# A new instruction order for pooled attention with two MLPs, and weight conversion held in SBUF

## The chip, the cores and the metric

The kernel runs on one core of a Trainium2 chip. The time is device microseconds of one execution, the median of several runs. PE is the matrix engine (TensorE), DVE is VectorE, ACT is ScalarE, POOL is GpSimd, and SP issues the transfers.

## The reference, cut to what matters

```python
# q (12288, 128), kv (384, 32, 128), w_sr (128, 128), all float32
kv_pool = kv.reshape(1, 96, 4, 8, 4, 128).mean(axis=(2, 4))    # 4x4 pooling: 768 keys
k = v = kv_pool.reshape(1, 768, 128) @ w_sr
s = (q @ k.T) / sqrt(128);  a = softmax(s);  x = a @ v         # x (12288, 128)

h = x @ moe_w_in                                               # (128, 2048), float64 in HBM
g = where(h >= 1, h, where(h <= -1, 0, (h + 1)**2 / 4))
x = g @ moe_w_out                                              # (2048, 128), float64 in HBM

h = x @ moe2_w_in
return (h * (1 / (1 + exp(-1.702 * h)))) @ moe2_w_out
```

The four MLP weights arrive as float64 and are turned into pairs of 32-bit values (a high part and the rest) on the chip.

## The kernel before

**Stages.** The 12288 queries are cut into 24 blocks of 512. At the start twelve chunks of kv of 512 KB are loaded (L265), four rows summed by DVE (even chunks, L277) or POOL (odd chunks, L280 and L281), and multiplied by a pooling matrix on PE (L294). The last two chunks, 10 and 11, are split: one half is summed by DVE, the other goes to PE unsummed in eight small matmuls (L292). The pooled keys, 768 columns in two halves of 384, are copied by ACT (L338), multiplied with w_sr (L343), and split into two parts kT by ACT (L350) and DVE (L210). The second half is done in two pieces: 256 columns that need chunk 9, and 128 columns that need chunk 11. Values are made by L368 and L376. While kv loads, PE also runs matmuls on a tile of zeros (`warm`, L320): 36 of 256 columns at the start and 7 after each of nine chunks.

**A block.** A block's attention is scores S (L214 to L216, six matmuls of 384 columns per tile of 128 queries), maximum (L523), exponential (L536), and the product with the values. Blocks 0 to 3 turn the probabilities on PE (L585) and multiply in plain float32 (L599); the others turn them by DVE and HBM. Then each MLP takes the 16 groups of 128 hidden columns in eight pairs: six matmuls into h, some elementwise work, a high part `ghi` by ACT and a rest `glo` by POOL (L210) or DVE, six matmuls into acc. In MLP 1 the elementwise work is a clip (L788 on DVE, or L786 on ACT where the block's digit in `LIGHT` isn't 0), a square (L795 on ACT, or L793 on POOL where the digit is 1) and L799 on DVE. MLP 2 uses two activations (L828, L834); its `glo` goes to DVE for the pairs named in `LOW_DVE` (pair 4 of every block).

**Weights.** Sixteen units of 128x512, four for each of W1, O1, W2, O2, are loaded (512 KB each) and converted (function `unit`): an absolute value on ACT into a tile `i`, a clamp (L413), a shift (L417), a sign (L421) and a tail (L428) on DVE, a high part on ACT (L435) and the rest on POOL (L210). Tile `i` lies in PSUM, in the one buffer of the room `accB`, and the result `f` of the tail in SBUF, in the room `o`, which has two buffers.

**The order.** Nothing is reordered at run time. `Plan` places every task with a list scheduler when the program is built: each engine, when it comes free, takes the ready task with the lowest key whose buffers ("rooms") are free. Keys and assumed durations are numbers in the code. The order that comes out is written into each engine's stream, and the engine keeps to it. Room `h` has three buffers of PSUM, shared by the scores, the transposes, the h of both MLPs, the key products and `warm`. The clamp of every weight unit is placed after all of kT (`after=[a, *kT_done]`).

Of the kernel before, what the change touches and what calls it, by code (L numbers as in the profile page):

```python
# [17 lines left out]
PSUM = bass.MemoryType.PSUM  # L18

# [111 lines left out]
def tile_pooled_attention_two_mlps(  # L131
# [40 lines left out]
    MM, MMS, MMF = 0.2273, 0.173, 0.224  # L172
# [4 lines left out]
    ATT_AT, ATT_GAP, REG_AT = ((-84.9, 56.1, 67.6, 104.1), ((2.4, 7.7), (8.6, 4.4), (9.6, 0.3), (2.5, 2.3)), 2.93)  # L177
    STEP_AT = (0.54, 2.45, 0.5)
    ATT_KEY = (26.49, 2.85, 18.08, 13.03, -19.64, 10.84, 4.1, -15.3, 8.86, 57.26, -2.82)
    PAIR1 = (3.65, -0.48, 3.27, 7.62, -6.74)  # L180
    PAIR2 = (1.57, -6.31, 2.52, 13.5)
    ENDS = (7.48, -5.42)
    V_AT = (-50, -16.8)
    LEAD = (-6.4, -20.7)
    LOW_DVE = (4,)
    LIGHT = ('12010111', '02111000', '22200000')
# [16 lines left out]
    def hold(room):  # L203
        return Hold(R[room])

# [22 lines left out]
    warm = sb.tile([P, 256], BF16, name="warm")  # L228
# [27 lines left out]
    pool_mm = [None] * NPC  # L256
    kv_rooms = ["u"] * 4 + ["hi"] * 4 + ["lo"] * 4
    pool_hold = [hold("accA"), hold("accB")]
    for i in range(NPC):
# [39 lines left out]
        if i >= NPC - 2:  # L299
            s = add("DVE", 1.05, -90 + i, lambda i=i, yh=yh: sums(nc.vector, i, yh, slice(0, 1)), after=[t], takes=[yh], uses=[h])  # L300
            direct = add("PE", 0.8, -90 + i, lambda i=i, f=pooled: f(i, [1], True), after=[t, c_t], uses=[h, ph])
            pool_mm[i] = add("PE", 0.23, -90 + i, lambda i=i, f=pooled: f(i, [0]), after=[s, c_t, direct], uses=[yh, ph])
        else:
            whole = slice(0, GP)
            if i % 2 == 0:
                s = add("DVE", 1.92, -90 + i, lambda i=i, yh=yh: sums(nc.vector, i, yh, whole), after=[t], takes=[yh], uses=[h])
            else:
                s = add("POOL", 2.05, -90 + i, lambda i=i, yh=yh: sums(nc.gpsimd, i, yh, whole), after=[t], takes=[yh], uses=[h])
            pool_mm[i] = add("PE", 0.45, -90 + i, pooled, after=[s, c_t], uses=[yh] + ([] if first else [ph]),
                             takes=[ph] if first else [])  # L310
# [3 lines left out]
    for i in range(NPC - 2):  # L314

        def work(i=i):
            if i == 0:
# [4 lines left out]
        add("PE", 5.0 if i == 0 else 0.43, 300, work, after=[w_t] if i == 0 else [pool_mm[i - 1]],  # L322
            uses=[warm_h] if i else [], takes=[] if i else [warm_h])
# [5 lines left out]
    def k_part(c0, c1, after):  # L329
        half = c0 // HALF  # L330
        fresh = c0 % HALF == 0
        r = slice(c0 % HALF, (c1 - 1) % HALF + 1)
        n = c1 - c0

        def copy():
            if fresh:
                pT_t[half] = slot(pT_h[half], [P, HALF], F32, "pT", "hi")
            nc.scalar.activation(pT_t[half][:, r], pool_ps[half][:, r], AF.Copy)  # L338

        def mult():  # L340
# [4 lines left out]
        a = add("ACT", act_us(n), -70 + half, copy, after=[after], uses=[pool_hold[half]] + ([] if fresh else [pT_h[half]]),  # L345
                takes=[pT_h[half]] if fresh else [])
        m = add("PE", 0.05 + n / 600, -80 + half, mult, after=[a, wsr_t], uses=[pT_h[half]] + ([] if fresh else [kps_h[half]]),
                takes=[kps_h[half]] if fresh else [])
        hi = add("ACT", act_us(n), -70 + half,
                 lambda: nc.scalar.activation(kT[0][:, c0:c1], kps_t[half][:, 0, r], AF.Copy), after=[m], uses=[kps_h[half]])  # L350
        lo = add("DVE", dve_us(n), -70 + half,
                 lambda: split_lo(nc.vector, kT[1][:, c0:c1], kps_t[half][:, 0, r], kT[0][:, c0:c1]),
                 after=[hi], uses=[kps_h[half]])
        kT_done.append(lo)
        kmul[half].append(m)
        return a
# [35 lines left out]
    def unit(name, src, j, rows, key, load_key, f_room):  # L392
# [32 lines left out]
        def tail():  # L425
            fi, raw = T["i", name, j].bitcast(I32), T["raw", name, j]
            f = T["f", name, j] = slot(fh, [P, TB], F32, "f")
# [14 lines left out]
        a = add("ACT", act_us(TB), key - 5, absolute, after=[d], uses=[rh], takes=[ih])  # L442
        b = add("DVE", 0.69, key - 4.5, clamp, after=[a, *kT_done], uses=[ih])
        c = add("DVE", 0.69, key - 4, shift, after=[b], uses=[ih])
        e = add("DVE", 0.69, key - 3.5, sign, after=[c], uses=[ih, rh])
        g = add("DVE", 0.69, key - 3, tail, after=[e], uses=[ih, rh], takes=[fh])
        hi = add("ACT", act_us(TB), key - 2, high, after=[g], uses=[fh], takes=[wh])
        lo = add("POOL", 1.3, key - 1, low, after=[hi], uses=[fh])
# [9 lines left out]
    for j in range(NW):  # L458
        unit("W1", w_in1, j, False, at(2 * j) - 2 - LEAD[0], -60 + 2 * j, "accB")
        unit("O1", w_out1, j, True, at(2 * j + LAG_O) - LEAD[0], -59 + 2 * j, "accB")  # L460
    for j in range(NW):
        unit("W2", w_in2, j, False, at(NP + LAG_B + 2 * j) - LEAD[1], -40 + 2 * j, "accB")
        unit("O2", w_out2, j, True, at(NP + LAG_B + LAG_O + 2 * j) - LEAD[1], -39 + 2 * j, "accB")

# [9 lines left out]
    def q_prep(b, key):  # L474
# [25 lines left out]
        d = add("SP", 2.0, key - 20 if b else -77, load, takes=[rh])  # L500
        a = add("DVE", 0.62, key - 5, turn, after=[d], uses=[rh], takes=[th, hh, lh])
        h = add("ACT", act_us(TB), key - 4, high, after=[a], uses=[th, hh])
        lo = add("POOL" if b else "DVE", 1.3 if b else 0.69, key - 3, low, after=[h], uses=[th, lh])
# [6 lines left out]
    def scores(b, t, key, ph=None, ahead=(1.0, 2.0, 2.5)):  # L510
# [3 lines left out]
        def S_mm():  # L514
            S = T["S", b, t] = psum(sh, f"S{b}_{t}")
            cols = [T[n, b][:, t * P : (t + 1) * P] for n in ("qhi", "qlo")]
            for half in range(2):
# [26 lines left out]
        m = add("PE", 6 * MMS, key, S_mm, after=[*kT_done, *q_done[b]], takes=[sh], uses=q_hold[b])  # L544
# [18 lines left out]
    def early(b, base, gap, gap2):  # L563
# [8 lines left out]
        def by_tile(n, t0, t1):  # L572
            return T[("pv", "spread", "rds")[n], b].rearrange("p (i t b) -> p i t b", i=4, b=32)[:, :, t0:t1, :]
# [201 lines left out]
    def pair1(b, k, a):  # L775

        t0 = at(a)
        hh, m = h_pair(1, b, k, t0)
# [38 lines left out]
        o_pair(1, b, k, at(a + LAG_O) + STEP_AT[1] * STEP, [hi, lo], [ih, lh])  # L817

    def pair2(b, k, a):

        t0 = at(a) + STEP_AT[0] * STEP
        hh, m = h_pair(2, b, k, t0)
        uh, ih, lh = hold("u"), hold("hi"), hold("lo")
        on_dve = k in LOW_DVE
# [24 lines left out]
        o_pair(2, b, k, at(a + LAG_O) + STEP_AT[2] * STEP, [hi, lo], [ih, lh])  # L849
# [79 lines left out]
```

## Time and profile before

| | |
|---|---|
| median of 3 runs | 1316.44 us (1315.85 to 1320.16) |
| the profiled execution: span from the first to the last instruction | 1315.1 us |
| PE busy | 1296.3 us (99%) |
| DVE, ACT, POOL busy | 932.6, 1089.0, 937.0 us |

The profiled execution has no time of its own beside its span; the median of the runs is 1.3 us longer than the span. PE is the engine to follow: its idle time, and work on it that serves nothing, are what a change of order can touch.

### The profile page before, as it was taken

To read this page: it belongs to the slowest core of one execution; us is meant where nothing else is said; L and a number is where in the kernel's file an instruction comes from. 1 tells how busy PE (TensorE), PEld (TensorE's weight loads), DVE (VectorE), ACT (ScalarE), POOL (GpSimd) and SP (SyncE) were. 2 spreads that over 40 slices of the span, in tenths; PEclk is the share of its full clock that TensorE was granted. 3 is DMA by queue.
4 is the path that set the end of the run, shared out by engine and by line. 5 is a ranking of instruction groups with operands and counts; after the bars stand their busy time and mean duration, and the time that the engine had idled before them with its cause. 6 is when DMAs were issued, how large, how long until landed. Compare 5 with 4: busy or idle time off the path is not lost.

```text
span 1315.1 us, 17281 instructions
## 1 busy us (share of the span) xinstructions
PE 1296.3 (99%) x6025; PEld 1088.1 (83%) x6025; DVE 932.6 (71%) x1196; ACT 1089.0 (83%) x1260; POOL 937.0 (71%) x427
## 2 busy tenths in 40 slices
PE   8899999999999999999999999999999999999998
PEld 7688788888888888888888888888888888888886
DVE  5887587777768777777777677777776877775531
ACT  2888888988888889888888898898888888987765
POOL 3577876776777667667767777677677766767886
PEclk8999999999999999999999999999999999999999
DMA  9400045534543454455345534554454345433000
GB/s 329 146 16 9 1 112 168 137 110 148 136 127 104 137 153 127 113 167 134 107 124 147 144 106 112 168 137 112 147 137 125 104 140 152 118 104 99 6 8 16
DMA packets 166309, 154.30 MB, mean 117 GB/s; under 512 B 108240, under 2 KB 153424, under 8 KB 166224
## 3 DMA queue, kind: packets, MB, share of 16 engines
q1 hardware_dynamic: 165168, 153.07, 41.2%
q8 instruction: 49, 0.80, 0.3%
q14 instruction: 36, 0.29, 0.1%
q10 hardware_dynamic: 1056, 0.13, 0.1%
HBM read 83.95 MB, written 69.21 MB: 116 GB/s over the span
## 4 chain that ended last, share of the span: by engine, by line
PE 95%; DVE 2%; DMA 1%; ACT 1%; issue 0%; POOL 0%; SPq 0%; DVEq 0%; ACTq 0%; POOLq 0%
PE acc L767 13%; PE acc L765 13%; PE acc L764 13%; PE h L214 13%; PE h L215 13%; PE h L216 13%; PE S L214 2%; PE S L216 2%; PE S L215 2%; PE pv L216 2%; PE pv L214 2%; PE pv L215 2%; PE pv L599 2%; DMA kv<-in_kv 1%; PE T L585 1%; DVE mx L523 0%
## 5 line engine op out<-in xcount | busy, mean ns | idle before, releaser
L210 POOL TENSOR_TENSOR glo<-u,ghi 128x1024 fp32r<-128x1024 f32 x360 | 860.3, 2408 | 303.5 <-ACT ghi L805 135.1
L788 DVE TENSOR_SCALAR u<-h 128x1024 f32<-128x1024 f32 x179 | 219.4, 1225 | 197.6 <-PE h L216 184.7
L764 PE MATMUL acc<-ghi,O 128*128 128x512 f32 x768 | 300.4, 391 | 0.0
L765 PE MATMUL acc<-ghi,O 128*128 128x512 f32 x768 | 299.6, 390 | 0.0
L799 DVE SCALAR_TENSOR_TENSOR u<-h,u 128x1024 f32<-128x1024 f32 x192 | 233.2, 1215 | 85.7 <-ACT u L795 80.9
L828 ACT ACTIVATE ghi<-h 128x1024 fp32r<-128x1024 f32 x192 | 197.2, 1027 | 71.4 <-PE h L216 70.7
L767 PE MATMUL acc<-glo,O 128*128 128x512 f32 x768 | 237.6, 391 | 0.0
L795 ACT ACTIVATE u<-u 128x1024 f32<-128x1024 f32 x184 | 194.5, 1057 | 31.7 <-DVE u L788 31.2
L805 ACT ACTIVATE ghi<-u 128x1024 fp32r<-128x1024 f32 x192 | 203.3, 1060 | 9.7 <-DVE den L540 3.9
L834 ACT ACTIVATE u<-h 128x1024 f32<-128x1024 f32 x168 | 171.2, 1020 | 0.0
L767 PEld LDWEIGHTS acc<-glo,O 128*128 128x128 f32 x768 | 144.0, 188 | 31.2 <-POOL glo L210 0.4
L765 PEld LDWEIGHTS acc<-ghi,O 128*128 128x128 f32 x768 | 144.2, 188 | 27.8
L764 PEld LDWEIGHTS acc<-ghi,O 128*128 128x128 f32 x768 | 144.1, 188 | 26.8
L214 PE MATMUL h<-xhi,W 128*128 128x512 f32 x384 | 150.3, 392 | 5.2 <-ACT xhi L556 2.3
L215 PE MATMUL h<-xlo,W 128*128 128x512 f32 x384 | 149.8, 390 | 0.2 <-DVE xlo L210 0.2
L214 PE MATMUL h<-x2hi,W 128*128 128x512 f32 x384 | 149.7, 390 | 0.1
L216 PE MATMUL h<-xhi,W 128*128 128x512 f32 x384 | 149.7, 390 | 0.0
L215 PE MATMUL h<-x2lo,W 128*128 128x512 f32 x384 | 149.4, 389 | 0.0
L216 PE MATMUL h<-x2hi,W 128*128 128x512 f32 x384 | 149.4, 389 | 0.0
L523 DVE TENSOR_REDUCE mx<-S 128x1 f32<-128x768 f32 x96 | 91.5, 953 | 8.7 <-PE S L216 6.4
L214 PEld LDWEIGHTS h<-xhi,W 128*128 128x128 f32 x384 | 72.1, 188 | 22.4 <-issue 2.5
L215 PEld LDWEIGHTS h<-xlo,W 128*128 128x128 f32 x384 | 72.1, 188 | 15.7 <-DVE xlo L210 0.5
(94 smaller groups left out, 1835.3 us busy)
## 6 DMA issues: line engine op xcount, KB each, us to landing
turned<-TT SPq DMA_DIRECT2D x80, 768.0 KB, 4.2
PT_hi<-turned SPq DMA_DIRECT2D x160, 192.0 KB, 3.8
PT_lo<-turned SPq DMA_DIRECT2D x160, 192.0 KB, 4.6
kv<-in_kv SPq DMA_DIRECT2D x12, 512.0 KB, 7.8
q<-in_q SPq DMA_DIRECT2D x96, 64.0 KB, 2.4
out<-o SPq DMA_DIRECT2D x94, 64.0 KB, 1.9
raw_W<-in_moe_w_in SPq DMA_DIRECT2D x8, 512.0 KB, 9.6
raw_O<-in_moe_w_out SPq DMA_DIRECT2D x8, 512.0 KB, 9.4
```

Of the source, the lines that this page charges most:

```text
L210: eng.tensor_tensor(out=lo, in0=full, in1=f32(hi), op=ALU.subtract)
L214: nc.tensor.matmul(ps, wl, xh, start=first, stop=False)
L215: nc.tensor.matmul(ps, wh, xl, start=False, stop=False)
L216: nc.tensor.matmul(ps, wh, xh, start=False, stop=last)
L764: nc.tensor.matmul(acc, w[c][1], hi[:, c], start=k == 0 and c == 0, stop=False)
L765: nc.tensor.matmul(acc, w[c][0], hi[:, c], start=False, stop=False)
L767: nc.tensor.matmul(acc, w[c][0], lo[:, c], start=False, stop=k == NP - 1 and c == 1)
L788: nc.vector.tensor_scalar(u, T["h", 1, b, k], -1.0, 1.0, ALU.max, ALU.add)
L795: nc.scalar.activation(u, u, AF.Square, scale=1.0 if light else 0.5)
L799: nc.vector.scalar_tensor_tensor(out=u, in0=T["h", 1, b, k], scalar=1.0, in1=u, op0=ALU.max, op1=ALU.min)
L805: nc.scalar.activation(t, T["u", b, k], AF.Copy)
L828: nc.scalar.activation(t, T["h", 2, b, k], AF.Gelu_apprx_sigmoid)
```

## The change

- All keys are moved into a table `ORDER`, and many have new values; some lists now have values for each of the first three to six blocks. Early attention has the keys (-143.62, 2.8, 71.1, 121.75) where it had (-84.9, 56.1, 67.6, 104.1).
- While kv loads: `warm` has 512 columns; 16 matmuls run at the start, 3 after each of the first nine chunks, and 2 after the direct matmuls of chunk 10, with a key ahead of most other work where before it was behind all. Pooling matmuls, key copies and key products get lower keys. The half sum of chunk 11 goes to POOL.
- Block 0's q is loaded by one transfer whose runs are 512 bytes (four transfers with runs of 128 bytes before), and transposed by four PE instructions into the second bank of the `warm` tile (one DVE transpose before). Its scores are two tasks for each tile; the first needs only the first half of kT.
- In the conversion of W1 and O1 the tile `i` lies in SBUF, in the room `o`, and the tail writes over it. The clamps of units 1 and 3 of each (`"1212"`) go to POOL. W2 and O2 keep PSUM.
- `LIGHT` and `LOW_DVE` have digits for five and six blocks: 13 squares on POOL (8 before), and 12 rests of MLP 2 on DVE in blocks 0 to 5 (6 before).

```diff
+    LOW_DVE=("00111011", "00001000", "11001000", "00000000", "00000001", "01000001"),
+    CONV=("1212", "1212", "0000", "0000"),
+    LIGHT=("10010111", "01111000", "02000000", "00000010", "00001101"),
...
-    LOW_DVE = (4,)
-    LIGHT = ('12010111', '02111000', '22200000')
...
         if i >= NPC - 2:
-            s = add("DVE", 1.05, -90 + i, lambda i=i, yh=yh: sums(nc.vector, i, yh, slice(0, 1)), after=[t], takes=[yh], uses=[h])
-            direct = add("PE", 0.8, -90 + i, lambda i=i, f=pooled: f(i, [1], True), after=[t, c_t], uses=[h, ph])
+            last_eng = "DVE" if i % 2 == 0 else "POOL"
+            s = add(last_eng, 1.05, -90 + i, lambda i=i, yh=yh, e=last_eng: sums(nc.vector if e == "DVE" else nc.gpsimd, i, yh, slice(0, 1)),
+                    after=[t], takes=[yh], uses=[h])
+            direct_mm[i] = add("PE", 0.9, -120 + i, lambda i=i, f=pooled: f(i, [1], True), after=[t, c_t], uses=[h, ph])
...
-            for _ in range(36 if i == 0 else 7):
-                nc.tensor.matmul(T["warm"][:, 0, :256], warm[:, :P], warm, start=True, stop=True)
-        add("PE", 5.0 if i == 0 else 0.43, 300, work, after=[w_t] if i == 0 else [pool_mm[i - 1]],
+            for _ in range(n):
+                nc.tensor.matmul(T["warm"][:, 0], warm[:, :P], warm, start=True, stop=True)
...
+    spare(16, -95, [w_t], first=True)
+    for i in range(NPC - 3):
+        spare(3, -95, [pool_mm[i]])
+    spare(2, -95, [direct_mm[NPC - 2]])
...
+        conv = ORDER["CONV"][("W1", "O1", "W2", "O2").index(name)][j]
+        in_sb, on_pool = conv != "0", conv == "2"
         def absolute():
-            f = T["i", name, j] = slot(ih, [P, TB], F32, "i")
+            f = T["i", name, j] = slot(fh if in_sb else ih, [P, TB], F32, "i")
         def clamp():
-            nc.vector.tensor_scalar(f, f, F64_LO, F64_HI, ALU.max, ALU.min)
+            (nc.gpsimd if on_pool else nc.vector).tensor_scalar(f, f, F64_LO, F64_HI, ALU.max, ALU.min)
...
+                nc.sync.dma_start(t, q[b * TB : (b + 1) * TB, :].rearrange("(t p) c -> p t c", p=P))
+            def turn():
+                T["qT", b] = T["warm"][:, 1]
+                for t in range(NT):
+                    nc.tensor.transpose(T["qT", b][:, t * P : (t + 1) * P], T["q", b][:, t, :], ident)
...
+        if b == 0:
+            m0 = add("PE", 3 * MMS, key, lambda: S_mm(range(1)), after=[kT_done[0], *q_done[b]], takes=[sh], uses=q_hold[b])
+            m = add("PE", 3 * MMS, key, lambda: S_mm(range(1, 2)), after=[m0, *kT_done], uses=[sh, *q_hold[b]])
```

## Rows read from the trace of the kernel before

**Rows 1.** Page, busy time of each engine over the span.
```profile
PE 1296.3 (99%) x6025; PEld 1088.1 (83%) x6025; DVE 932.6 (71%) x1196; ACT 1089.0 (83%) x1260; POOL 937.0 (71%) x427
```

**Rows 2.** Windows: stretch, length, busy time by engine, granted clock, DMA share, GB/s.
```profile
40.00:50.00 10.00, 7.52 (x45) 6.01 (x42) 7.32 (x12) 5.70 (x10) 4.15 (x3) 1.00 0.65 181
50.00:60.00 10.00, 7.47 (x40) 6.50 (x41) 9.63 (x15) 9.21 (x13) 7.97 (x5) 1.00 0.07 11
60.00:80.00 20.00, 18.02 (x115) 15.99 (x113) 16.28 (x30) 15.97 (x24) 17.72 (x11) 1.00 0.09 14
80.00:100.00 20.00, 18.51 (x100) 15.32 (x99) 16.34 (x28) 16.48 (x25) 15.03 (x9) 1.00 0.09 14
100.00:150.00 50.00, 48.65 (x278) 41.92 (x278) 38.73 (x58) 43.20 (x58) 39.82 (x22) 1.00 0.04 6
200.00:250.00 50.00, 49.51 (x223) 41.26 (x223) 37.26 (x48) 43.09 (x49) 36.00 (x16) 1.00 0.45 119
400.00:500.00 100.00, 100.00 (x452) 84.02 (x451) 73.87 (x90) 86.14 (x98) 71.75 (x31) 1.00 0.49 135
```

**Rows 3.** Windows of one us behind the last kv chunk, same columns.
```profile
21.00:22.00 1.00, 1.00 (x7) 1.00 (x6) 1.00 (x2) 0.00 (x0) 0.00 (x0) 0.50 0.83 188
27.00:28.00 1.00, 1.00 (x8) 1.00 (x7) 0.00 (x0) 0.00 (x0) 0.00 (x0) 0.64 1.12 396
```

**Rows 4.** Timeline, kv chunks and q: start, duration, instruction, idle time before it.
```profile
10.05 5.73 SPq L480 DMA_DIRECT2D q<-in_q  x4
13.87 1.27 POOL L280 TENSOR_TENSOR z<-kv 128x512 f32<-128x512 f32 x1 [0.46 <-DMA kv<-in_kv]
16.35 1.27 POOL L280 TENSOR_TENSOR z<-kv 128x512 f32<-128x512 f32 x1 [0.40 <-DMA kv<-in_kv]
18.84 1.08 PE L292 MATMUL pool_ps<-pm,kv 128*128 128x32 f32 x8 [0.54 <-DMA kv<-in_kv]
```

**Rows 5.** Chain that ended last, from chunk 11 on: start, duration, what.
```profile
20.66 1.75 PE pool_ps L292 x8
22.44 0.39 ACT pT L338
22.87 1.22 PE k_ps L343 x2
24.36 2.99 PE warm_ps L320 x14
27.35 0.43 PE k_ps L343 x2
27.77 0.71 PE k_ps L368 x6
28.82 0.29 DVE kT L210
29.11 0.62 DVE i L413
29.75 0.70 DVE i L417
43.48 0.69 DVE i L421
```

**Rows 6.** Timeline, block 1's scores: what came before them.
```profile
46.79 0.70 DVE L487 STREAM_TRANSPOSE qT<-q 128x512 f32<-128x512 f32 x1
50.25 1.28 POOL L210 TENSOR_TENSOR qlo<-qT,qhi 128x512 fp32r<-128x512 f32 x1
52.53 0.41 PE L214 MATMUL S<-kT,qlo 128*128 128x384 f32 x1 [2.54 <-DVE u L799]
```

**Rows 7.** Groups by line and shape: count, busy us, mean ns, idle before.
```profile
L413 DVE TENSOR_SCALAR i<-i 128x512 f32<-128x512 f32 x16 | 11.1, 691 | 2.1 <-ACT i L409 2.1
L210 POOL TENSOR_TENSOR glo<-u,ghi 128x1024 fp32r<-128x1024 f32 x360 | 860.3, 2408 | 303.5 <-ACT ghi L805 135.1 <-ACT u L834 119.6 <-ACT u L795 25.3
L793 POOL TENSOR_TENSOR u<-u 128x1024 f32<-128x1024 f32 x8 | 15.2, 1895 | 5.9 <-ACT u L786 5.9
```

More of the change, by code (lines that the diff above doesn't have):

```diff
@@ L204, in hold, with by_block @@
         return Hold(R[room])
+    def by_block(name, b):
+        return ORDER[name + "E"][b] if b < len(ORDER[name + "E"]) else ORDER[name]
     def f32(ap):
@@ L255, in tile_pooled_attention_two_mlps @@
     pool_ps, pT_t, kps_t = {}, {}, {}
-    pool_mm = [None] * NPC
+    pool_mm, direct_mm = [None] * NPC, {}
     kv_rooms = ["u"] * 4 + ["hi"] * 4 + ["lo"] * 4
@@ L441, in unit @@
         d = add("SP", 1.3, load_key, load, takes=[rh], lag=3.0)
[L442 to L448, printed above, removed]
+        k0, k1, k2, k3, k4, k5, k6 = (key + u for u in ORDER["UNIT"])
+        th = fh if in_sb else ih
+        a = add("ACT", act_us(TB), k0, absolute, after=[d], uses=[rh], takes=[th])
+        b = add("POOL" if on_pool else "DVE", 1.29 if on_pool else 0.69, k1, clamp, after=[a, *kT_done], uses=[th])
+        c = add("DVE", 0.69, k2, shift, after=[b], uses=[th])
+        e = add("DVE", 0.69, k3, sign, after=[c], uses=[th, rh])
+        g = add("DVE", 0.69, k4, tail, after=[e], uses=[th, rh], takes=[] if in_sb else [fh])
+        hi = add("ACT", act_us(TB), k5, high, after=[g], uses=[fh], takes=[wh])
+        lo = add("POOL", 1.3, k6, low, after=[hi], uses=[fh])
         wh.left += 1
@@ L498, in low, with load @@
             split_lo(nc.gpsimd if b else nc.vector, t, T["qT", b], T["qhi", b])
[L500 to L503, printed above, removed]
+        if b == 0:
+            def load():
+                t = T["q", b] = slot(rh, [P, NT, C], F32, f"q{b}")
+                nc.sync.dma_start(t, q[b * TB : (b + 1) * TB, :].rearrange("(t p) c -> p t c", p=P))
[3 more added lines that the diff above has]
+                    nc.tensor.transpose(T["qT", b][:, t * P : (t + 1) * P], T["q", b][:, t, :], ident)
+            d = add("SP", 0.7, -77, load, takes=[rh], lag=2.6)
+            a = add("PE", 0.5, -125, turn, after=[d, c_t], uses=[rh, warm_h], takes=[hh, lh])
+            h = add("ACT", act_us(TB), -98, high, after=[a], uses=[warm_h, hh])
+            lo = add("DVE", dve_us(TB), -98, low, after=[h], uses=[warm_h, lh])
+        else:
+            d = add("SP", 2.0, key - 20, load, takes=[rh])
+            a = add("DVE", 0.62, key - 5, turn, after=[d], uses=[rh], takes=[th, hh, lh])
+            h = add("ACT", act_us(TB), key - 4, high, after=[a], uses=[th, hh])
+            lo = add("POOL", 1.3, key - 3, low, after=[h], uses=[th, lh])
         q_done[b], q_hold[b] = [h, lo], [hh, lh]
@@ L512, in scores, with S_mm @@
         sh = hold("h")
-        def S_mm():
-            S = T["S", b, t] = psum(sh, f"S{b}_{t}")
+        def S_mm(halves=range(2)):
+            if 0 in halves:
+                T["S", b, t] = psum(sh, f"S{b}_{t}")
+            S = T["S", b, t]
             cols = [T[n, b][:, t * P : (t + 1) * P] for n in ("qhi", "qlo")]
-            for half in range(2):
+            for half in halves:
                 mm3(S[:, half, :HALF], cols, [k[:, half * HALF : (half + 1) * HALF] for k in kT], True, True)
```

84 lines of the change are left out of this document (52 added, 32 removed).

## The prediction

> **What bounds the kernel now.** I read the page first, for the engine that matters, then the windows, for the place where that engine loses time, and then the chain and the timeline at that place. PE is busy for 1296.3 of 1315.1 us [rows 1], and no other engine comes near it. So the time can only fall by what PE loses: time idle, time at half clock, and matmuls that serve nothing. The windows say where that is. From 400 to 500 us PE shows 100.00 of 100 [rows 2], and there is nothing to win; the loss lies ahead of 250 us, where the windows leave PE 2.48, 2.53, 1.98, 1.49, 1.35 and 0.49 us idle, in their order [rows 2]. Ahead of 40 us stands the loading of kv, where a busy PE says little, because much of what it does there is filler on a tile of zeros.
>
> In the chain, chunk 11 of kv is the last thing that a transfer ends: its direct matmuls start at 20.66, and DVE ends the last piece of kT at 28.82 + 0.29 = 29.11 [rows 5]. Those 8.45 us hold little that chunk 11 itself needs. Fourteen filler matmuls take 2.99 of them; a copy and a product of the other 256 columns, which wait for chunk 9 alone, take 0.39 + 1.22, and a hand-over between them makes 1.65; the value products take 0.71 ahead of the key copy [rows 5]. The clock is part of it: the eight direct matmuls of chunk 10 took 1.08 us [rows 4], those of chunk 11 took 1.75 [rows 5], and the granted clock is 0.50 (1.2 GHz) in 21 to 22 us and 0.64, so on its way back to 2.4 GHz, in 27 to 28 [rows 3].
>
> The reader has to know one limit of what follows. The diff gives keys, and the order that they make is not written in it. So I price each stage by what its rows leave to win, from nothing to all, and choose inside.
>
> **The end of the kv load.** POOL's waits for chunks 7 and 9 ended at 13.87 and 16.35, so chunks came 1.24 us apart; chunk 10 came 2.49 us later and chunk 11 another 1.82 [rows 4, 5]. At the earlier pace chunk 11 would have been there at 16.35 + 2.48 = 18.83, 1.83 us sooner. What falls into that time is block 0's q, four transfers that SP spent 5.73 us on [rows 4], in 2048 runs of 128 bytes. The change leaves its place on SP behind kv and makes it 512 runs of 512 bytes. The bytes stay, and nothing shows whether the runs or the bytes delayed kv: the gain lies between 0 and 1.83. I take 1.2, because the earlier pace is the nearest row of transfers with long runs, and q's own bytes still have to pass. SP is also free sooner for the sixteen weight loads behind it, which costs nothing.
>
> **From chunk 11 to kT.** The filler behind the ninth chunk no longer runs behind all other work, and none follows chunk 11, so the 2.99 us should leave the chain. The 1.65 us of the 256 columns leave it if the order puts them ahead of chunk 11's direct matmuls; their keys are lower now. The 0.71 of the value products can leave too. So 0 to 2.99 + 1.65 + 0.71 = 5.35; nothing at all only if other work takes the filler's place. I take the filler whole and half of the 1.65: 3.8. The half sum of chunk 11 on POOL instead of DVE, and q's transposes on PE instead of DVE, cost nothing: POOL and DVE both wait for that chunk, and q is ready before kT.
>
> **The clock.** If PE kept its full clock there, the three pieces still in the chain (1.75, 0.43 and 0.71 [rows 5]) would gain some 1.2 us. If it falls as before and no filler is there to raise it, PE's next work, block 0's attention, runs at half clock for up to as long as the low stretch lasted, 21 to 27.6 [rows 3], and half of 6.6 us, 3.3, is lost. Between -1.2 and +3.3 I take 0.
>
> **From kT to block 0's x.** On the chain, the clamp (0.62 of it), the shift (0.70) and one sign (0.69) of weight units stand ahead of steps of block 0's softmax [rows 5]. That is 2.0 us. They are there because DVE was free when they were ready, and a lower key for attention doesn't stop that; I take 0.5 of 0 to 2.0.
>
> **Idle time of PE behind that.** Most of the 2.48 us of 40 to 50 is the wait for that x (at 43.48 the chain is on DVE [rows 5]), which moves with it and is not counted. The rest is 2.53 + 1.98 + 1.49 + 1.35 + 0.49 = 7.84 [rows 2]. One piece is 2.54 long: scores of block 1 at 52.53, whose last operand came from POOL at 50.25 + 1.28 = 51.53 and whose PSUM came from DVE [rows 6]. Its q was turned at 46.79; the key of that attention falls from 56.1 to 2.8, which puts it ahead of the first MLP's elementwise work. I take 2.5 for it. The other 5.3 us are many small waits, and a new order can as well add as remove: I take 1.0. Together 3.5, of 0 to 7.84.
>
> **The conversion in SBUF.** Eight units of W1 and O1 no longer queue for one PSUM buffer. Four clamps of 0.691 us leave DVE [rows 7], 2.8 us, and come to POOL. No row shows a POOL clamp; the nearest are two-input sums of 512 elements, 1.27 [rows 4], and half of a 1.895 us square of 1024 [rows 7], 0.95. So POOL gets 3.8 to 5.1 us, and I take 1.27 each, 5.1. Behind a clamp on POOL stand the rests `glo` of 2.41 us that PE's output matmuls wait for; POOL was busy 17.72 of 20 us in 60 to 80 [rows 2], so there up to 1.3 us may be late once for each clamp, and in return the six rests more that go to DVE take 6 x 2.41 = 14.4 us off POOL, and five more squares bring 5 x 1.895 = 9.5 us back. On balance POOL is at 5.1 + 9.5 - 14.4, about 0. DVE takes those six rests at no more than twice a clamp, 6 x 1.38 = 8.3 us over the time of six blocks, some 300 us, where it is idle a quarter of the time (73.87 of 100 [rows 2]). None of this is on PE, and I take 0 for it; its bounds are a gain of the 2.8 us of DVE, in 50 to 60 where DVE is busy 9.63 of 10 [rows 2], and the loss in the fourth rival.
>
> The clamp took 0.691 us with its tile in PSUM [rows 7], and no row shows one in SBUF. The Trainium skill ("VectorE: DVE Perf Modes", section "The perf-mode tier table (the rule you actually need)") says that such an instruction on float32 makes two results per cycle when both sides are in SBUF, and not with PSUM. By it the four clamps left on DVE and the eight shifts would take some 0.42 us, an estimate from that page, and DVE would be spared 12 x 0.27 = 3.2 us more; the sum for PE stays the same by either.
>
> **The sum.** 1.2 + 3.8 + 0 + 0.5 + 3.5 = 9.0 us less: a span of 1306.1 against 1315.1. The median of the runs stood 1.34 us above the profiled span, so 1307.4, which I round to 1307. This kernel's time can be told from no change from about 0.3% on, 3.9 us.
>
> **The rivals.** *The holes close as well.* If the early order is good enough for PE never to wait, the other 4.3 us of holes and the other 1.5 us of conversions go too: 1307.4 - 5.8 = 1301.6. For it speaks that no engine is full from 60 to 150 (DVE 71.35, ACT 75.65 and POOL 72.57 of 90 [rows 2]); against it, that each wait is short and of another kind. Chance 0.17.
>
> *The clock stays low and q still delays kv.* 1307.4 + 3.3 + 1.2 = 1311.9. For it: there is less filler behind chunk 10 than before. Against: q's transposes and first halves of scores fill PE at that place. Chance 0.08.
>
> *The others don't follow.* PE starts sooner and meets work that isn't ready, because in 50 to 60 DVE is full, and converting weights and block 1's softmax both need it. Then the end moves by what DVE loses only, 2.8 us, to 1313.6, within 0.3%. For it: 9.63 of 10 [rows 2]. Against: a kT that is ready 5 us sooner lets DVE begin sooner too. Chance 0.09.
>
> *Slower: DVE waits for POOL.* With `i` in SBUF, sign and tail of eight units read two tiles of SBUF; before, one of the two was in PSUM. If such an instruction can't run beside a POOL instruction, 16 of them meet rests of 2.41 us on an engine that is busy 0.8 of the time from 60 to 150 [rows 2, 7]: half a rest each, 16 x 1.2 x 0.8 = 15.4 us of DVE, which in a full DVE go to PE's path: 1307.4 + 15.4 = 1322.8. It decides from 9 us, 0.56 us for each, on. No row of the trace before has DVE in this form beside a busy POOL. Against: DVE has time to spare from 60 on (32.6 of 40 us busy to 100 [rows 2]). Chance 0.06. The Trainium skill ("SBUF — State Buffer", section "Who interferes with whom") states this rule: a DVE instruction with two inputs in SBUF and a GpSimd instruction that reads SBUF share a port, and the second blocks until the first ends; no run here shows it yet.
>
> **How the numbers follow.** The forecast, with 1303 to 1312 as its own range, has what is left, 0.60. The first two rivals with it are faster: 0.85. The third is the same, 0.09, and the fourth slower, 0.06. The range of 8 in 10 goes down to 1300, a little under the first rival, and up to 1314, past the second and third; it leaves out the fourth and extremes.
>
> **What would show it.** In the changed profile, chunk 11 lands near 19.5 us, and no filler stands in the chain behind it. The last piece of kT ends near 24. The first scores start near 24 and block 0's x by 40. From 50 to 150 PE's idle time falls from 7.35 to some 4 us, and from 250 us on the windows are as before. Sign and tail of W1 and O1 last 0.69 as before; if they last over a microsecond where POOL is busy, the fourth rival is there. A granted clock of 0.50 past 25 us would show the second. The prediction is wrong if kT comes 5 us sooner and the last matmul does not, or if PE has new idle time behind 150 us.

## The result, and the profile after

The changed kernel takes 1330.13 us (median of 4 runs, 1328.18 to 1330.57), the kernel before 1318.3 (4 runs beside them, 1315.85 to 1320.48): a ratio of 1.0091, with an interval of 1.0075 to 1.0107. It is slower by 0.9%, where I forecast 0.7% faster. It is the side of the fourth rival, which had 0.06. The profiled execution took 1328.18 us, the shortest of the four, and has a span of 1326.4, 11.3 longer than before.

The page, busy time of each engine, beside [rows 1]:

```profile
PE 1299.0 (98%) x5973; PEld 1084.6 (82%) x5975; DVE 944.1 (71%) x1195; ACT 1084.6 (82%) x1256; POOL 943.1 (71%) x432
```

PE is busy 2.7 us more, with 52 fewer matmuls on record, and idle for 27.4 us (1326.4 - 1299.0) where it was 18.8 (1315.1 - 1296.3). So of the 11.3 us, 8.6 are new idle time. The windows, in the stretches and columns of [rows 2], say where:

```profile
40.00:50.00 10.00, 5.51 (x39) 4.65 (x38) 7.94 (x12) 4.41 (x8) 5.97 (x4) 0.92 0.24 40
50.00:60.00 10.00, 7.49 (x33) 5.95 (x32) 9.12 (x13) 7.12 (x10) 6.37 (x5) 0.91 0.09 15
60.00:80.00 20.00, 15.09 (x63) 11.78 (x61) 19.53 (x21) 12.00 (x16) 18.31 (x10) 0.91 0.00 0
80.00:100.00 20.00, 17.16 (x114) 15.34 (x115) 15.58 (x25) 14.13 (x22) 18.64 (x11) 1.00 0.09 14
100.00:150.00 50.00, 46.93 (x282) 41.10 (x282) 40.64 (x67) 39.97 (x57) 35.60 (x21) 1.00 0.07 11
200.00:250.00 50.00, 50.00 (x227) 41.98 (x227) 36.89 (x45) 43.35 (x50) 33.91 (x15) 1.00 0.48 133
400.00:500.00 100.00, 100.00 (x451) 83.81 (x450) 75.67 (x97) 85.75 (x99) 69.01 (x31) 1.00 0.48 134
```

From 40 to 150 PE is idle 4.49 + 2.51 + 4.91 + 2.84 + 3.07 = 17.8 us; before it was 2.48 + 2.53 + 1.98 + 1.49 + 1.35 = 9.8 [rows 2]. That is 8.0 of the 8.6. The 2.7 us of busy time go with a lower clock: 0.92, 0.91 and 0.91 were granted in the three stretches from 40 to 80, where it was 1.00 [rows 2]. From 200 on there is nothing. The worst stretch is 60 to 80: PE runs 63 instructions where it ran 115, and DVE, 16.28 of 20 busy before, is busy 19.53, though it runs fewer instructions (21 for 30). So its instructions take longer on average.

The conversion of the weights shows which ones do. Groups by line, operation and shape of DVE, with count, busy time and mean ns; L446 is the clamp, L450 the shift, L454 the sign, L461 the tail:

```profile
L450 DVE TENSOR_SCALAR i<-i 128x512 int32<-128x512 int32 x16 | 16.1, 1006 | 1.1 <-POOL i L446 1.0
L454 DVE SCALAR_TENSOR_TENSOR i<-raw_O,i 128x512 int32<-128x512 int32 x8 | 8.4, 1052 | 0.1
L454 DVE SCALAR_TENSOR_TENSOR i<-raw_W,i 128x512 int32<-128x512 int32 x8 | 7.8, 989 | 0.1
L446 DVE TENSOR_SCALAR i<-i 128x512 f32<-128x512 f32 x12 | 7.2, 608 | 0.3 <-ACT i L442 0.3
L461 DVE SCALAR_TENSOR_TENSOR i<-raw_O,i 128x512 int32<-128x512 int32 x4 | 4.6, 1146 | 0.0
L461 DVE SCALAR_TENSOR_TENSOR i<-raw_W,i 128x512 int32<-128x512 int32 x4 | 3.0, 762 | 0.1
```

With the eight tails of W2 and O2, which still read PSUM (5.4 us), 60 instructions take 52.5 us. Before, the clamp was 0.691 [rows 7], and in the same view the 64 of all four kinds took 44.0, 0.688 each; 60 at that price are 41.3. So DVE does the same work in 11.2 us more. The means hide two kinds of instruction; shortest, median and longest, in ns, by the view of tile `i`:

```profile
L450 DVE TENSOR_SCALAR i<-i x16: 419/699/2609, 29.4 to 147.3; 128x512 int32<-128x512 int32 x16
L446 DVE TENSOR_SCALAR i<-i x12: 383/686/699, 28.8 to 146.6; 128x512 f32<-128x512 f32 x12
L454 DVE SCALAR_TENSOR_TENSOR i<-raw_O,i x8: 673/696/2772, 34.6 to 140.2; 128x512 int32<-128x512 int32 x8
L446 POOL TENSOR_SCALAR i<-i x4: 1908/1950/2355, 39.7 to 94.3; 128x512 f32<-128x512 f32 x4
```

These rows mix two places of the tile. Of the 16 shifts, and of the 12 clamps on DVE, eight are of W2 and O2, whose tile is still in PSUM. Which is which follows from DVE's order, which the run with one-input instructions below shares. Taken one by one in the timeline, the 32 instructions of W2 and O2 took 0.67 to 0.70 us. Of those in SBUF, the eight shifts took 0.42, 0.88, 0.43, 1.51, 1.11, 1.04, 2.61 and 2.57, the four clamps 0.42, 0.42, 0.38 and 0.56, and of the 16 signs and tails nine took 0.67 to 0.69 and seven 0.95 to 2.77. The timeline of DVE and POOL says what the long ones have in common (start, duration, instruction):

```profile
58.89 5.22 POOL L232 TENSOR_TENSOR glo<-u,ghi 128x1024 fp32r<-128x1024 f32 x2 [2.81 <-ACT ghi L864]
61.78 0.69 DVE L446 TENSOR_SCALAR i<-i 128x512 f32<-128x512 f32 x1
62.38 2.29 DVE L461 SCALAR_TENSOR_TENSOR i<-raw_O,i 128x512 int32<-128x512 int32 x1
...
75.09 2.83 POOL L232 TENSOR_TENSOR glo<-u,ghi 128x1024 fp32r<-128x1024 f32 x1
75.60 2.61 DVE L450 TENSOR_SCALAR i<-i 128x512 int32<-128x512 int32 x1
...
96.20 4.91 POOL L232 TENSOR_TENSOR glo<-u,ghi 128x1024 fp32r<-128x1024 f32 x2
96.27 2.57 DVE L450 TENSOR_SCALAR i<-i 128x512 int32<-128x512 int32 x1 [0.39 <-POOL i L446]
98.88 2.77 DVE L454 SCALAR_TENSOR_TENSOR i<-raw_O,i 128x512 int32<-128x512 int32 x1
```

The two rests `glo` on POOL run from 96.20 to 101.11, and two DVE instructions, a shift of 0.42 and a sign of 0.69 when nothing holds them up, fill 96.27 to 101.65 beside them, one for each rest. The shift that starts at 75.60 ends at 78.21; the rest beside it, which had started 0.51 us before it, ends at 77.92. This is so each time. Of the 28 DVE instructions on W1 and O1, twelve began while a POOL instruction with two inputs was under way, and every one outlasted it: the six shifts ended 0.28 to 0.29 us after it, the four signs and two tails 0.55 us after it. So it looks as if they had stood still until POOL was done. The place of the tile decides: the clamp at 61.78, which has its tile in PSUM, takes 0.69 beside the same rest that holds up the tail at 62.38. POOL pays too: the rest at 75.09 took 2.83, where the mean was 2.41 [rows 7]; a sign that had begun at 73.55 ran until 75.68 beside it. The Trainium skill ("SBUF — State Buffer", section "Who interferes with whom") says that a DVE instruction with two SBUF inputs and a GpSimd instruction that reads SBUF use one shared port, that a `tensor_scalar` on SBUF can take the same port, and that the later one blocks until the first is through; these rows agree. Beside POOL's clamps, which read one tile, the rows differ from it: three DVE instructions on W1 and O1 began beside one, took 0.56, 0.69 and 0.98 us, and were through before it.

How that reaches PE, on ACT at the end of block 0's attention and on PE at its first product of MLP 1:

```profile
44.99 0.63 ACT L468 ACTIVATE W<-i 128x512 fp32r<-128x512 f32 x1 [2.85 <-DVE i L461]
45.53 0.58 ACT L679 ACTIVATE rds<-pv 128x512 f32<-128x512 f32 x1
...
48.24 0.61 PE L236 MATMUL h<-xhi,W 128*128 128x512 f32 x1 [4.42 <-issue]
```

ACT keeps its written order, so `rds`, a step of the attention, stands behind the high part of a weight unit, and that waits 2.85 us for a tail, in whose chain stand a clamp of 2.35 us on POOL (39.69 to 42.04) and a sign of 1.64 us (42.54). The matmul that follows starts at 48.24, after 4.42 us of idle PE. Before, it started at 45.21, after 2.31:

```profile
45.21 0.47 PE L214 MATMUL h<-xhi,W 128*128 128x512 f32 x1 [2.31 <-ACT xhi L556]
```

The start of the kernel, kv and q, beside [rows 4]:

```profile
17.81 1.08 PE L314 MATMUL pool_ps<-pm,kv 128*128 128x32 f32 x8
19.08 0.72 POOL L302 TENSOR_TENSOR z<-kv 128x256 f32<-128x256 f32 x1 [0.47 <-DMA kv<-in_kv]
19.79 0.66 PE L544 MATMUL warm_ps<-ident,q 128*128 128x128 f32 x4 [0.90 <-DMA q<-in_q]
20.87 1.69 PE L314 MATMUL pool_ps<-pm,kv 128*128 128x32 f32 x8
```

Chunk 11 is there at 19.08; I forecast 19.5. But PE has q's transposes ahead of it and waits 0.90 us for q, and so the direct matmuls of chunk 11 start at 20.87, later than the 20.66 before [rows 5]. The chain that ended last, beside [rows 5] (start, us, what):

```profile
24.52 0.43 PE warm_ps L345
25.17 2.77 PE warm_ps L345 x6
27.93 0.28 PE k_ps L373 x2
...
73.64 2.04 DVE i L454
75.68 2.53 DVE i L450
...
96.27 2.58 DVE i L450
98.88 2.77 DVE i L454
```

The filler is still in it, 0.43 + 2.77 = 3.20 us where it was 2.99, ahead of the last key product, and with the clock at half:

```profile
22.00:23.00 1.00, 0.56 (x3) 0.42 (x2) 0.00 (x0) 0.40 (x2) 0.00 (x0) 0.50 0.99 390
27.00:28.00 1.00, 1.00 (x5) 0.64 (x4) 0.00 (x0) 0.00 (x0) 0.00 (x0) 0.53 1.00 405
```

The last piece of kT ends at 28.85 (28.56 + 0.29); before it was 29.11, and I forecast 24.

### The profile page after: what moved, and what is told of

Read it like the earlier page. It is cut to its first block, busy times and chain, and to the rows that moved or that the text cites. A ratio compares the mean times of both kernels' runs of the same rounds, so it can differ in the third digit from the quotient of the medians.

```text
span 1326.4 us, 17158 instructions
## 1 busy us (share of the span) xinstructions
PE 1299.0 (98%) x5973; PEld 1084.6 (82%) x5975; DVE 944.1 (71%) x1195; ACT 1084.6 (82%) x1256; POOL 943.1 (71%) x432
## 4 chain that ended last, share of the span: by engine, by line
PE 93%; DVE 3%; POOL 1%; DMA 1%; issue 1%; ACT 0%; SPq 0%; ACTq 0%; POOLq 0%
PE h L237 13%; PE acc L823 13%; PE acc L822 13%; PE acc L825 13%; PE h L236 13%; PE h L238 13%; PE S L236 2%; PE S L238 2%; PE S L237 2%; PE pv L237 2%; PE pv L238 2%; PE pv L236 2%; PE pv L657 1%; DMA q<-in_q 1%; DVE i L450 1%
## 5 line engine op out<-in xcount | busy, mean ns | idle before, releaser
L232 POOL TENSOR_TENSOR glo<-u,ghi 128x1024 fp32r<-128x1024 f32 x354 | 847.3, 2412 | 309.4 <-ACT ghi L864 146.9
L854 ACT ACTIVATE u<-u 128x1024 f32<-128x1024 f32 x179 | 189.4, 1058 | 29.8 <-DVE u L847 29.4
L894 ACT ACTIVATE u<-h 128x1024 f32<-128x1024 f32 x162 | 165.1, 1020 | 0.0
L237 PEld LDWEIGHTS h<-xlo,W 128*128 128x128 f32 x384 | 72.3, 188 | 15.4 <-DVE xlo L232 0.5
```

Source lines behind the costliest of these rows:

```text
L232: eng.tensor_tensor(out=lo, in0=full, in1=f32(hi), op=ALU.subtract)
L237: nc.tensor.matmul(ps, wh, xl, start=False, stop=False)
L854: nc.scalar.activation(u, u, AF.Square, scale=1.0 if light else 0.5)
```

## The experiments

Two theories stood first. *A*: DVE instructions with their tile in SBUF, and POOL's instructions, hold each other up, and this costs the 12 us. *B*: the new order, or POOL's clamps, costs them. Behind these stood the other question, why the 9.0 us of gain did not come. Of the later theories, *E* says that block 1's q holds the end in place when kT comes sooner, and *F* that nothing ahead of kT is on the path that sets the end; others are told in the expectations in which they come up.

**The change without its conversion.** `CONV` all zero; the keys of the weights as before, with `W_AT` all zero; all else of the new order stays.

```diff
-    LEAD=(38.93, 13.93),
-    UNIT=(-81.37, 33.9, 137.81, 22.85, 55.09, 191.43, 11.04),
-    CONV=("1212", "1212", "0000", "0000"),
+    LEAD=(-6.4, -20.7),
+    UNIT=(-5, -4.5, -4, -3.5, -3, -2, -1),
+    CONV=("0000", "0000", "0000", "0000"),
```

> The changed kernel with the conversion as before: tile i of W1 and O1 in PSUM, no clamp on POOL, and the old keys of the weight units; all else of the new order stays. Theory A (DVE and POOL hold each other up when the tile lies in SBUF): sign, tail, clamp and shift last 0.69 us each again, and the time falls from 1330 by some 10 us or more, to 1310 to 1320. Theory B (the rest of the new order is the loss: block 0's x comes at 48 us instead of 45): it stays at 1326 to 1332.

1324.05 us, 1.0042 (1.0027 to 1.0057). The conversion's instructions are back at 0.67 to 0.70 us, so the stretching goes with the tile in SBUF. The time lies between the theories: this kernel has an order of its own, planned anew from mixed keys.

**All clamps on DVE.** `CONV=("1111", "1111", "0000", "0000")`.

> The changed kernel with all clamps on DVE, tile i of W1 and O1 still in SBUF. Theory A, with shifts, signs and tails as the cause: DVE instructions up to 2.7 us remain and the time is 1322 to 1330. Theory A', with the four POOL clamps of 1.9 to 2.4 us (1.29 in the plan) as the cause: 1312 to 1320. Theory B: 1326 to 1332.

1335.81 us, 1.0139 (1.0122 to 1.0155): slower still, above every range that I had set, in an order planned anew, with tails of up to 2.4 us. So it isn't POOL's clamps that the stretching needs.

**Only the tile moved.** The kernel before, with `i` of W1 and O1 in SBUF and nothing else.

```diff
-            f = T["i", name, j] = slot(ih, [P, TB], F32, "i")
+            f = T["i", name, j] = slot(fh if in_sb else ih, [P, TB], F32, "i")
...
-            f = T["f", name, j] = slot(fh, [P, TB], F32, "f")
+            f = T["f", name, j] = T["i", name, j] if in_sb else slot(fh, [P, TB], F32, "f")
```

> The kernel before with one thing of the change: tile i of W1 and O1 in SBUF, in room o, the tail writing over it; clamps stay on DVE, keys as they were. Theory A: some signs, tails, clamps and shifts are stretched from 0.69 to as much as 2.7 us, and the time grows by 3 to 10 us, to 1320 to 1328. Theory B: within 0.3% of the kernel before, or faster, since two units can be under way.

1336.16 us, 1.0139 (1.0124 to 1.0154), beyond theory A's 1328, with the same picture, by the view of tile `i` (L418 is the shift, L429 the tail):

```profile
L418 DVE TENSOR_SCALAR i<-i x16: 405/685/2505, 32.2 to 135.2; 128x512 int32<-128x512 int32 x16
L429 DVE SCALAR_TENSOR_TENSOR i<-raw_O,i x4: 681/1166/2267, 37.9 to 83.6; 128x512 int32<-128x512 int32 x4
```

The edit that takes nothing from the order's keys makes the kernel slower by 18 us. But the planner made a new order from it, since the room `o` is now held longer, and so this run doesn't tell what of the 18 is stretching.

**The same with instructions of one input.** A reduction over one element takes the place of clamp, shift, sign and tail of W1 and O1 in the kernel above.

```diff
+        def alone():
+            f = T["i", name, j]
+            nc.vector.tensor_reduce(f, f.rearrange("p (n o) -> p n o", o=1), AX.X, ALU.max)
```

> The kernel before with tile i of W1 and O1 in SBUF and the order that follows from it, and its clamps, shifts, signs and tails for these weights replaced by the one-input maximum, so that this arithmetic is left out. It differs from the earlier run with the tile in SBUF (1.39% slower) by the collisions alone. Theory A: it is back within 0.3% of the kernel before, or faster. If the order that follows from the SBUF tile was at fault there: 0.8% slower or more.

1328.44 us, 1.0078 (1.0061 to 1.0094). Of the 18 us, 7.7 go with the stretching, and 10.4 stay with no stretching left, so they are put down to the order that the planner made. So a change of the planner's input can cost as much as the whole matter here, and the runs that decide keep every engine's order.

**The changed kernel, order kept, DVE's conversion by one input.** The function above in place of DVE's 28 instructions on W1 and O1 (12 of them clamps and shifts, 16 signs and tails); the four clamps on POOL stay.

> The changed kernel with its exact order; the DVE clamps, shifts, signs and tails of W1 and O1 are replaced by a maximum over one element of the same tile, one SBUF input and 0.69 us as planned, so that the conversion's arithmetic is left out for these two weights. Theory A: none of these lasts over 0.75 us, POOL's clamps come nearer to 1.3, and the time falls by 8 us or more, to 1312 to 1322. Theory B: the order is the same, so 1326 to 1332.

1318.89 us, 1.0008 (0.9999 to 1.0018). Tile `i` (L458 is the shift in PSUM), the first product of block 0's MLP, and two windows:

```profile
L446 DVE TENSOR_REDUCE i<-i x28: 644/676/689, 27.1 to 90.4; 128x512 f32<-128x512 f32 x28
L458 DVE TENSOR_SCALAR i<-i x8: 679/695/700, 37.1 to 136.2; 128x512 int32<-128x512 int32 x8
L452 POOL TENSOR_SCALAR i<-i x4: 1906/1914/1921, 38.0 to 86.9; 128x512 f32<-128x512 f32 x4
```

```profile
45.42 0.47 PE L236 MATMUL h<-xhi,W 128*128 128x512 f32 x1 [3.28 <-issue]
```

```profile
60.00:80.00 20.00, 17.02 (x79) 13.62 (x78) 15.64 (x28) 16.06 (x25) 20.00 (x12) 0.91 0.05 8
100.00:150.00 50.00, 50.00 (x291) 44.02 (x291) 37.30 (x54) 41.65 (x55) 38.67 (x20) 1.00 0.05 8
```

None of the 28 takes over 0.689 us, beside a POOL that is busy 20.00 of 20 in 60 to 80. DVE falls from 19.53 to 15.64 there, PE's idle time from 40 to 150 falls from 17.8 to 9.7 us (9.8 before), and the time is 11.2 us less (10.9 by the ratios, 0.0083 of 1318; their intervals together leave some 2.5 either way). The first product of block 0's MLP starts at 45.42 in place of 48.24, but not by this alone: 1.7 us of it stood already at kT (27.19 for 28.85), in a profile with a granted clock of 1.00 in 20 to 22, where the changed kernel's had 0.78. This is theory A by itself: with the order, the tile's place and POOL's clamps as they were. The Trainium skill ("SBUF — State Buffer", section "Who interferes with whom") says that a `tensor_reduce` never contends with GpSimd on trn2; the 28 rows agree.

**Which instructions.** The same function for signs and tails alone, and for DVE's clamps and shifts alone.

> The changed kernel with its exact order; only signs and tails of W1 and O1 (two SBUF inputs) are replaced by the one-input maximum, so their arithmetic is left out; clamps and shifts stay as they are. If two-input instructions are what collides, 1317 to 1321. If clamps and shifts, which last 0.42 us where POOL is idle, collide as much, the gain is half: 1322 to 1327.

> The changed kernel with its exact order; only clamps on DVE and shifts of W1 and O1 are replaced by the one-input maximum, so their arithmetic is left out; signs and tails stay. If clamps and shifts collide as much as signs and tails, 1322 to 1327. If two-input instructions are the whole cause, 1327 to 1332.

Without two-input instructions 1321.33 us, 1.0028 (1.0017 to 1.0038); without clamps and shifts 1328.1, 1.0078 (1.0063 to 1.0094). Against 1330.13 that is 8.8 and 2.0. The 2.0 can't be told from nothing, since the interval reaches 1.0094 and the changed kernel stands at 1.0091. So most of the time goes with the two-input instructions, as that theory had it (1328.1 lies in its 1327 to 1332, 1321.33 just above its 1317 to 1321). The shifts alone still leave 2.4 us over the 1318.89 of the run with neither. The two don't simply add: what is left in each kernel still stretches. Without the shifts, the 16 signs and tails are held up more, 21.0 us together where they took 18.4; without the signs and tails, the eight shifts in SBUF take 10.2 where they took 10.6. The rows are the shifts of the first kernel (eight of the 16 in PSUM) and the tails of the second:

```profile
L454 DVE TENSOR_SCALAR i<-i x16: 419/700/2576, 29.3 to 140.2; 128x512 int32<-128x512 int32 x16
```

```profile
L469 DVE SCALAR_TENSOR_TENSOR i<-raw_O,i x4: 675/1632/2626, 35.4 to 97.9; 128x512 int32<-128x512 int32 x4
```

**The start: q by long runs.** With the stretching away, the new order is worth nothing (1.0008). The next runs look for its gain. First the kernel before, with block 0's q as in the change.

```diff
+                nc.sync.dma_start(t, q[b * TB : (b + 1) * TB, :].rearrange("(t p) c -> p t c", p=P))
...
+                    nc.tensor.transpose(T["qT", b][:, t * P : (t + 1) * P], T["q", b][:, t, :], ident)
...
+            a = add("PE", 0.5, -125, turn, after=[d, c_t], uses=[rh, warm_h], takes=[hh, lh])
```

> The kernel before with block 0's q as in the change: one transfer with runs of 512 bytes, four transposes on PE into the second bank of the filler's tile, and scores in two tasks a tile. Theory C: chunk 11 lands 1.2 to 1.8 us sooner, at 18.8 to 19.4, and the time falls by 1 to 2 us. Theory D': PE reaches the transposes ahead of chunk 11's work in its order and waits for q there, so the gain is lost: within 0.1%.

1324.58 us, 1.0052 (1.004 to 1.0065), slower than either theory had it, in an order planned anew. PE waits for q here as well, 0.80 us, ahead of chunk 11.

**The start: less filler.** The kernel before, without the filler behind the eighth and ninth chunk.

```diff
-    for i in range(NPC - 2):
+    for i in range(NPC - 4):
```

> The kernel before without the fillers behind chunks 7 and 8, the fourteen matmuls of 2.99 us that stand in its chain ahead of the last key product; nothing else. Theory C (what stands between chunk 11 and kT is on the path to the end): kT is ready 2 to 3 us sooner, at 26 to 27 us, and the time falls by 1.5 to 3 us. Theory D (filler only fills half-clock time, and what follows hides it): the clock stays at 0.50 for longer, the scores run at half speed, and the time is within 0.1% of the kernel before.

1317.36 us, 1.0 (0.9991 to 1.0009). The last key product starts at 25.04 (27.14 before), kT is done at 27.72 (29.11), and block 0's MLP starts at 43.82 (45.21): 1.4 us sooner. Then it is lost; rows of DVE, of the windows and of PE show how it went:

```profile
46.73 0.71 DVE L487 STREAM_TRANSPOSE qT<-q 128x512 f32<-128x512 f32 x1 [1.23 <-DMA q<-in_q]
```

```profile
44.00:48.00 4.00, 3.84 (x10) 2.79 (x10) 2.37 (x4) 2.19 (x4) 1.61 (x2) 0.62 0.17 30
```

```profile
52.76 0.41 PE L214 MATMUL S<-kT,qlo 128*128 128x384 f32 x1 [2.54 <-DVE u L799]
```

The clock is granted at 0.62 in 44 to 48, so part of the time at 1.2 GHz, where it was 1.00; DVE waits 1.23 us for block 1's q; and block 1's scores start at 52.76, where they started at 52.53 [rows 6].

**Block 1's q sooner.** Was it that wait? Its load ahead of the weights of MLP 2, by key (with and without the filler of the last run):

```diff
-        d = add("SP", 2.0, key - 20 if b else -77, load, takes=[rh])
+        d = add("SP", 2.0, (-41 if b == 1 else key - 20) if b else -77, load, takes=[rh])
```

> The kernel before with block 1's q loaded ahead of the weights of MLP 2 instead of behind them; nothing else, though the whole order follows from it. Theory E (the stretch from 46 to 53 us hangs on this q, which is behind 8.4 MB of weights): it is turned 5 us or more sooner than at 46.79, the wait of 2.5 us at 52.5 goes, and the time falls by 1 to 3 us. Rival: DVE, busy 9.6 of 10 us there, is the limit anyway: within 0.15% of the kernel before.

> Both: no filler behind chunks 7 and 8, and block 1's q ahead of the weights of MLP 2. Theory E: what the filler's removal brought (kT 1.4 us sooner) is no longer eaten by the wait for that q, and the time falls by 2.5 to 4.5 us. Rival (DVE is the limit): within 0.15%.

1329.74 us, 1.0089 (1.0074 to 1.0104), and 1330.54, 1.0096 (1.0079 to 1.0114). One key of one load made 12 us. This tells of the planner, not of q.

**The same with the order kept.** Only the one load is moved in SP's stream, first alone, then with less filler (the key products' order stays as it was).

```diff
-    for t in plan.order():
+    order = plan.order()
+    order.remove(loads["q", 1])
+    at_w = order.index(loads["W2", 0])
+    at_q = order.index(turns_q[0]) + 1
+    order.insert(max(at_w, at_q), loads["q", 1])
+    for t in order:
```

```diff
-            for _ in range(36 if i == 0 else 7):
+            for _ in range(36 if i == 0 else 7 if i < 8 else 0):
```

> The kernel before, every engine's order as it was, with one exception: on SP block 1's q is issued ahead of the first weights of MLP 2 instead of behind the last. Theory E (46 to 53 us waits for this q): little alone, because block 0's x at 45.8 us comes no sooner; 0 to 1 us faster. Rival (DVE is the limit): within 0.1%. Slower only if the weights of MLP 2, some 0.6 us later, are missed.

> As the run beside it, and the fourteen filler matmuls ahead of the last key product left out, the order otherwise untouched. Theory E: kT and x come 1.4 us sooner, q is there, and the end comes 1.2 to 2 us sooner. Rival (the stretch is bound by DVE, or by PE's half clock after a longer idle time): within 0.1% of the kernel before.

1317.78 us, 0.9999 (0.999 to 1.0008), and 1317.04, 0.9993 (0.9983 to 1.0003). The load does what it should (in the first of the two q is turned at 46.48 with no wait), and the end stays. The second kernel's profiled execution shows one way in which the gain goes:

```profile
28.00:32.00 4.00, 4.00 (x15) 4.00 (x14) 2.99 (x6) 2.45 (x5) 1.83 (x1) 0.52 1.04 399
```

Block 0's scores run at half clock (0.52; it was 1.00 in the kernel before in the same stretch), and block 0's MLP starts at 45.64, later than before. This execution is the longest of the eleven (1320.12 us), and its last kv chunk was there at 21.39, 0.7 us later than in the profile before, so it shows what can happen and not the usual course.

**The changed kernel with less filler, order kept.** Its eight late filler matmuls left out.

```diff
-        spare(3, -95, [pool_mm[i]])
-    spare(2, -95, [direct_mm[NPC - 2]])
+        spare(3, -95, [pool_mm[i]], left_out=i >= 7)
+    spare(2, -95, [direct_mm[NPC - 2]], left_out=True)
```

> The changed kernel, every engine's order as it was, without the filler that still stands ahead of its last key product (eight matmuls of 512 columns). Theory F (what stands ahead of kT is not on the path, DVE's collisions behind it are): kT comes 1.5 to 3 us sooner and the time stays within 0.15% of the changed kernel's 1330. Theory C: it falls by as much as kT moves, to 1327 to 1328.5.

1329.58 us, 1.0093 (1.0079 to 1.0106): no change against the changed kernel's 1.0091. The last key product starts at 24.52, where it was 27.73. The last piece of kT ends at 25.91 instead of 28.85, and block 0's MLP starts at 47.27 instead of 48.24. So F fits both kernels as far as their times can tell; E falls, since q came without a wait and the end stayed.

None of these kernels is faster than the one before by anything that can be told.

## Why the prediction was wrong

**The conversion in SBUF: this step failed.** I took 0, with the loss left to the fourth rival at 0.06; by the run with one-input instructions it is 11.2 us. The rival's mechanism was right, its place in part: I had 60 to 150, and the hold-ups lie between 37 and 102. Its price was 15.4, from 16 instructions of two inputs held up for 1.2 us in 0.8 of cases. Seven of the 16 were held up, by 7.5 us together (durations of 1.64, 0.98, 1.53, 2.29, 2.13, 0.95 and 2.77, less 0.69 each): 1.1 each, nearly as priced, but fewer. The rest came from where I had expected a saving: the shifts, with one input. Two of the eight in SBUF took 0.42 and 0.43 us, as I had estimated from the Trainium skill ("VectorE: DVE Perf Modes", section "The perf-mode tier table (the rule you actually need)"). The six others, which began beside POOL, took 0.88 to 2.61, so that the eight cost 5 us more than at 0.69 and not 2.2 less. That the rival's 15.4 lies near the 11.2 is in part luck, since it had nothing for the shifts. I cited one half of what the Trainium skill says of the port ("SBUF — State Buffer", section "Who interferes with whom": two inputs) and left out the other (an instruction in a mode that uses both ports takes it too).

What made me give it 0.06 was the argument that DVE has time to spare from 60 on. It was the wrong question. Averaged, it had: 16.28 of 20 us [rows 2]. But an instruction that is held up delays what is queued behind it at once, and all queues are in a fixed order: a tail late by some 3 us held ACT's high part, that held the attention's `rds`, and PE stood still for 4.42 us, where it had waited 2.31. And the spare time was 3.7 us in that stretch, of which 3.3 were used.

**The order's gains: 0 instead of 9.0.** With the order kept and the stretching gone, the time is that of the kernel before (1.0008). By its terms:

- *End of the kv load, 1.2:* the size was about right. POOL's wait for chunk 11 ended at 19.08; before, DVE's ended at 20.71, so it is 1.6. It didn't reach the path, since PE waited for q first. I had asked whether q is ready before kT, and not whether it is ready before chunk 11's matmuls, ahead of which PE turns it.
- *From chunk 11 to kT, 3.8:* wrong. I took the filler out of the chain because it was no longer keyed behind all other work. But an engine takes the lowest key among what is ready: the last key product was still waiting for its copy, the filler was ready, and 3.20 us of it stood in between once more. With the wait for q, kT came 0.26 us sooner (28.85 for 29.11), where these two terms had 5.0. For these few tasks the keys in the diff might have told the order.
- *The clock, 0:* about right. The granted clock is 0.50 from 22 to 27 in both kernels, and 0.53 in 27 to 28, where it was 0.64. So my sign of the second rival, 0.50 past 25 us, told nothing: the kernel before shows it too.
- *kT to x, 0.5:* it went the other way. In the kernel without stretching, block 0's MLP starts 18.2 us after kT (45.42 less 27.19), where it was 16.1. The high part of a weight unit stands ahead of `rds` on ACT there too, and waits for its tail:

```profile
42.17 0.63 ACT L480 ACTIVATE W<-i 128x512 fp32r<-128x512 f32 x1 [1.94 <-DVE i L446]
```

- *Holes, 3.5:* the one hole that I named did close. Block 1's first scores start without a wait, at 51.22 in the changed kernel and at 48.54 without stretching, where they waited 2.54 [rows 6]. But others opened: without stretching PE is idle 3.63 us in 40 to 50, 2.08 in 50 to 60, 2.98 in 60 to 80, 1.00 in 80 to 100 and none in 100 to 150, 9.7 together where it was 9.8.
- *That a sooner kT moves the end at all:* the kernels with less filler say no. In the kernel before, 1.4 us at kT were gone at 53 us; in the changed kernel, 2.9 us at kT were 1.0 at block 0's MLP and nothing that can be told at the end. In both, a stretch of block 0's scores or of its MLP ran at a lower granted clock than in the kernel with the filler.
- *POOL's clamp, 1.27:* 1.91 us where DVE doesn't hold it up (four of 1.906 to 1.921, with the conversion on one input), half as much again as the two-input sum that I took it from. It doesn't count in the sum: the order with it, free of stretching, costs nothing.

**What stays open.** What binds the kernel before between 46 and 53 us isn't settled: neither block 1's q alone, nor the filler alone, nor both move the end. The half clock was seen, and not taken away by itself. That it is the port, and not another resource that POOL and DVE share, rests on the Trainium skill ("SBUF — State Buffer", section "Who interferes with whom"); the runs show which instructions are held up, beside which, and until when. No run puts the tile back into PSUM with the order kept; the units of W2 and O2 beside it stand in for that. Why POOL's clamps hold DVE up so little isn't known. A conversion in SBUF that doesn't meet POOL's instructions was not tried.

## What to carry to other kernels

Before an operand of a DVE instruction is moved from PSUM to SBUF, look at what GpSimd does at that time, and price each meeting with an instruction of two inputs at what is left of it, on the queue behind it and not on the average of the engine. Before a median is read, see whether its group mixes places of the operand. In a kernel whose order is written when it is built, an edit that lets the planner run again can move the time by 10 us by itself; test a suspected cost with every engine's order held fixed. A gain at the start is not yet a gain: here 1.4 and 2.9 us at kT came to nothing at the end, so look in the trace for the next thing that ends late.

## What was not expected of the hardware

- A shift of 128x512 with its tile in SBUF took 0.42 us by itself and up to 2.61 beside POOL; with its tile in PSUM it took 0.68 to 0.70 whatever POOL did.
- A DVE instruction on SBUF that met a POOL instruction of two inputs ended a fixed time after it, 0.28 to 0.29 us (shift) or 0.55 us (sign and tail), in twelve of twelve cases. Beside POOL's clamps, three of three were through before them.
- A clamp with two operations on POOL took 1.91 us for 128x512, more than POOL's two-input sum of that size (1.27 [rows 4]).
- In the changed kernel the granted clock fell after 4.42 us of idle PE at 48.24 (0.54 in 50 to 52) and after 2.37 us at 72.47 (0.58 in 72 to 74, 0.57 in 74 to 76), so to 1.2 GHz for most of it. After 2.84 us idle at 103.98 it was 1.00 in 104 to 106. The length of the last wait alone doesn't say whether it falls.
- With block 0's q in four transfers of 128-byte runs the last kv chunk, issued ahead of it, was there at 20.71 us, with one transfer of 512-byte runs at 19.08. All profiles that show the wait for this chunk fall into these groups: 20.32 to 21.89 in eight, 18.77 to 19.20 in seven. Whether it is the length of the runs or the number of transfers isn't told apart.
